# Dense products on scaled fp16 pairs instead of fp32r pairs, in an attention and MLP block on one core

## The chip, the cores and the metric

The kernel runs on one core of one Trainium2 chip. The time is device microseconds of one execution; the median of three runs is given. The core's engines work side by side, each through its own list of instructions in order: PE (matrix products into PSUM), ACT (functions with a scale and a bias), DVE (vectors), POOL (vectors, slower), and SP, which here issues all DMAs. They wait for each other by semaphores.

## The reference

```python
x  = A_x                                   # 1 x 2048 x 640, fp32
xn = _layernorm(x)
# attention, 32 heads of 20, each query sees itself and the 255 keys before it
qkv = (xn @ wqkv).reshape(1, 2048, 3, 32, 20)          # wqkv 640 x 1920
p = softmax(where(mask, (q @ k.T) * 20 ** -0.5, -1e9))
s = (p @ v).reshape(1, 2048, 640) @ wo                 # wo 640 x 640
# MLP on the same xn: w1 640 x 1536, w2 1536 x 640
r = relu(xn @ w1 + b1)
g = silu(r * r @ w2 + b2)
return x + s * g
```

All inputs and the output are fp32.

## The kernel before

**Pairs.** A dense product `a @ b` in fp32 is made of three PE products. Each operand is split into a high part, a rounded copy, and a low part, what is left of it; high x high, high x low and low x high are summed in PSUM. Before, both parts are `F32R` (fp32r, four bytes an element). ACT makes the high part (`AF.Copy`), DVE or POOL the low one (`tensor_sub`). The attention's own products (scores, values) use bf16 and fp16 parts and are not touched.

**Layout.** P = 128. The 2048 rows are NB = 4 blocks of BT = 512, NT = 16 tiles of 128. D = 640 is KC = 5 chunks of 128; F = 1536 is 12 chunks. `xT[p][b]` holds part p of the normalized, transposed x of block b. Large tiles come from the pool `bigp` (8 buffers of 128 x 2560 fp32).

**First stage** (lines 96 to 409). Block by block: x is loaded and normalized (`stats` L142, `normalize` L151), turned by PE (`tps`, L167 and L302), split into `xT` (L103, L104) and spilled to DRAM (`spill_x`). From it come k and q of head group 0 (`qk_group` L201, `qk_evac`), and v for all heads (`v_all`: products `vps` L243 of 320 columns, evacuated into `vt` by ACT L247 and L251 and DVE L248 and L252). The weights wv and the first wq, wk groups are split by ACT (L178) and POOL (L179).

**Attention stage.** 16 head pairs x 16 query tiles make 256 steps, written out in the loop at the end of the function. Step s issues the scores of one tile (`sps` L432) and their row maxima (DVE, `junk` L444), nine steps later the transposed scores (`stps` L476), exponentials (ACT L483), the window's edges (POOL L484, L486), the fp16 high part (ACT L491) and low part (DVE L497), and later the value products (`ops` L511). Between these, `fill()` takes dense products out of a generator, `filler()`, as many as a table of costs per product allows (`total`, `per`), so that they are spread evenly over the steps:

- q and k of groups 1 to 4: `qkps` L562, 480 products of 512 columns, evacuated at L734 to L739 into three staging tiles from `stgp` (8 buffers) and stored to `q_d`, `k_d`;
- the MLP in two halves of F, `hf` = 0, 1. For each half the 8 blocks of MT = 256 rows: the split x is loaded back (`load_xb`, tile `xb`), `hps` (L562) multiplies it with w1, ACT and DVE make the squared relu, POOL its low part (`hh`, L785), `yps` (L816, 320 columns) multiplies with w2. The first half's result goes to DRAM (`y_d[0]`) and is loaded and added in the second (`yin`).

Weights for the fill pass through `piece`, which loads a raw tile and splits it some steps later, one per step (`tick`); `ensure(tag)` forces the rest of a tag.

**Last stage.** The attention's output is turned and split (`oT`), multiplied with wo (`wops` L562, 320 columns), multiplied with silu(y) and added to x.

All engines are under `manual_schedule`: the order of the code is the order of each engine's list. Within a `v_all` tile the code is

```python
for c in range(KC):
    for xp, wp in ((0, 0), (0, 1), (1, 0)):
        n += 1
        nc.tensor.matmul(ps, xT[xp][b][:, ...], wv[wp][:, c, ...], ...)   # L243
nc.scalar.activation(dst[:, :, :, 0:DH], psv, AF.Copy)                     # L247
nc.vector.tensor_sub(r1, psv, dst[:, :, :, 0:DH])                          # L248
if late:
    late.pop()()            # the tile before: L251, L252
late.append(rest)
for _ in range(...):
    if jobs:
        jobs.pop(0)()       # statistics and normalization of block b + 2
```

Of the kernel before, what the change touches and what calls it, by code (L numbers as in the profile page):

```python
# [8 lines left out]
F32R = mybir.dt.float32r  # L9
# [5 lines left out]
P = 128  # L15
# [14 lines left out]
NFH = F // 2 // P  # L30
FHALF = F // 2
# [13 lines left out]


def f32(ap):
    return ap.bitcast(F32)
# [3 lines left out]
def attn_mlp_kernel(ctx: ExitStack, tc, x, wqkv, wo, w1, b1, w2, b2, out):  # L52
# [3 lines left out]
    bigp = ctx.enter_context(tc.tile_pool(name="bigp", bufs=8))  # L56
# [4 lines left out]


    xs_d = [[dram.tile([P, KC * BT], F32, name=f"xs{p}_{b}") for b in range(NB)] for p in range(2)]
# [12 lines left out]
    y_d = [dram.tile([P, NT, D], F32, name=f"y{i}") for i in range(2)]  # L76
# [21 lines left out]
    nc.gpsimd.memset(eps, EPS)  # L98
    b1t = const.tile([P, F // P], F32, name="b1t")
# [7 lines left out]
    xT = [[None] * NB for _ in range(2)]  # L107
# [19 lines left out]
    with tc.tile_pool(name="ph1v", bufs=2) as p1v, tc.tile_pool(name="ph1", bufs=2) as p1, tc.tile_pool(name="ph1x", bufs=4) as p1b, tc.tile_pool(name="ph1w", bufs=1) as p1w:  # L127
# [8 lines left out]

        wv = [p1w.tile([P, KC, D], F32R, name=f"wv{p}") for p in range(2)]

# [6 lines left out]
        def inv_std(rstd, var):  # L145
            nc.scalar.activation(rstd, var, AF.Sqrt, bias=eps)
            nc.vector.reciprocal(rstd, rstd)
# [5 lines left out]

        def alloc_x(b):
            for p in range(2):
                xT[p][b] = bigp.tile([P, KC * BT], F32R, tag="big", name=f"xT{p}_{b}")

        def spill_x(b):
            for p in range(2):
                nc.sync.dma_start(xs_d[p][b], f32(xT[p][b]))  # L160

        def transpose_chunks(b, xns):
            for c in range(KC):
# [4 lines left out]
                split(xT[0][b][:, c * BT:(c + 1) * BT], xT[1][b][:, c * BT:(c + 1) * BT], ps)  # L168
# [8 lines left out]
        def split_w(hi, lo, raw):  # L177
            nc.scalar.activation(hi, raw, AF.Copy)  # L178
            nc.gpsimd.tensor_sub(lo, raw, f32(hi))  # L179

        def group_tiles(g, w):
            return tuple(wgt.tile([P, KC, P], F32R, tag=f"wg{w}{q}", name=f"wg{w}{q}_{g}") for q in "hl")
# [12 lines left out]
        def qk_group(w, b, ps, t0=0, n=BT):  # L195
            hi, lo = ws0[w]
            m = 0
            for c in range(KC):
                for wt, part in ((hi, 0), (hi, 1), (lo, 0)):
                    m += 1  # L200
                    nc.tensor.matmul(ps, wt[:, c, :], xT[part][b][:, c * BT + t0:c * BT + t0 + n], start=m == 1, stop=m == 3 * KC)  # L201

        def qk_evac(w, b, ps, t0=0, n=BT):
# [3 lines left out]
            nc.scalar.activation(hm[:, 0, :], ps, AF.Copy)  # L207
            nc.vector.tensor_sub(rest, ps, hm[:, 0, :])
# [20 lines left out]
        def v_all(b, between=None):  # L229
            late = []  # L230
            jobs = norm_jobs(b + 2) if b + 2 < NB else []
            for nh in range(2):
# [3 lines left out]
                nc.gpsimd.memset(vt[:, :, :, :, VW - 1:VW], 1.0)  # L236
                for t in range(4):
                    ps = pmm.tile([P, HALF], F32, tag="mm", name="vps")
                    n = 0
                    for c in range(KC):  # L240
                        for xp, wp in ((0, 0), (0, 1), (1, 0)):
                            n += 1
                            nc.tensor.matmul(ps, xT[xp][b][:, c * BT + t * P: c * BT + (t + 1) * P], wv[wp][:, c, nh * HALF:(nh + 1) * HALF], start=n == 1, stop=n == 3 * KC)  # L243
# [12 lines left out]
                    for _ in range(0 if between and not nh else 2 if between else 1):  # L256
                        if jobs:
                            jobs.pop(0)()
                    store_all()
# [4 lines left out]
        with tc.manual_schedule(engines={E_.PE, E_.Activation, E_.DVE, E_.Pool, E_.SP}):  # L264
# [5 lines left out]
            ws0, ws1 = {}, {}  # L270
# [7 lines left out]
            views = [xT[p][0].rearrange("p (c n) -> p c n", c=KC) for p in range(2)]  # L278
            stats(xts[0][0], mv[:, 0, :])
            wjobs = []  # L280
            for w in "kq":
                ws0[w] = group_tiles(0, w)
                wjobs.append((*ws0[w], raws.pop(0)))
            firsts, seconds = [], []

            wvt = [bigp.tile([P, KC * BT], F32, tag="big", name=f"wvr{j}") for j in range(2)]
            wvr = [wvt[c // 3][:, c % 3 * D:(c % 3 + 1) * D] for c in range(KC)]
            for c in range(KC):
                nc.sync.dma_start(wvr[c], wqkv[c * P:(c + 1) * P, 2 * D:3 * D])
                wjobs.append((wv[0][:, c, :], wv[1][:, c, :], wvr[c]))  # L290

            def root(t):
                nc.scalar.activation(rstd[:, t:t + 1], mv[:, t, 1:2], AF.Sqrt, bias=eps)
# [16 lines left out]
            def rests(r):  # L310
                for ps, (hi, lo) in r:
                    nc.vector.tensor_sub(lo, ps, f32(hi))
# [16 lines left out]
            highs(t0_)  # L329
            stats(xts[0][2], mv[:, 2, :])  # L330
            root(2)
            rests(t0_)
            split_w(*wjobs.pop(0))
            t2_ = turned(2)
            highs(t1_)
            rests(t1_)
            split_w(*wjobs.pop(0))
# [7 lines left out]
            split_w(*wjobs.pop(0))  # L345
            highs(t3_)
            for _ in range(2):
                split_w(*wjobs.pop(0))
# [4 lines left out]
            for t in range(4):  # L353
                stats(xts[1][t], mv1[:, t, :])
# [5 lines left out]
            for f in firsts + seconds:  # L360
                if wjobs:
                    split_w(*wjobs.pop(0))
                lasts.append(qk_evac(*f))
                if len(lasts) == 2:
                    lasts.pop(0)()
            lasts.pop()()
            store_all()
            spill_x(0)
            nc.sync.dma_start(b1t, b1.rearrange("(c p) -> p c", p=P))
            nc.sync.dma_start(b2t, b2.partition_broadcast(P))  # L370
            ones_rows(0)
            for b in range(NB):
                def next_x():
                    if b + 1 < NB:
# [4 lines left out]
                        spill_x(b + 1)  # L379

                if b == 0:
                    inv_std(rstd1, mv1[:, :, 1])
                    xns = [normalize(xts[1][t], mv1[:, t, :], rstd1[:, t:t + 1]) for t in range(4)]
                    load_x(2)
                    raws = [load_w(group_src(1, w), KC) for w in "qk"]
                    v_all(b, next_x)
# [8 lines left out]
                next_x()  # L395
                if b == 1:
                    for w in "qk":
                        ws1[w] = group_tiles(1, w)
                        split_w(*ws1[w], raws.pop(0))
# [5 lines left out]
                v_all(b)  # L405
# [627 lines left out]
```

## Time and profile before

| | |
|---|---|
| median of 3 runs | 936.42 us (935.34 to 936.46) |
| profiled execution, first to last instruction | 933.0 us |
| PE busy | 907.9 us (97%) |
| DVE busy | 758.8 us (81%) |
| ACT busy | 670.1 us (72%) |
| POOL busy | 538.1 us (58%) |
| first stage | 0 to 120 us |
| attention stage with its fill | 120 to 852 us |
| last stage | 852 to 933 us |

No time is given for the profiled execution beside its span; the span is what its rows add up to. In a row of the profile `yps<-w,hh 128*128 128x320 f32 x1152 | 227.3, 331` means: 1152 products into `yps` with 128 rows and 320 columns, 227.3 us busy in all, 331 ns each from start to end. Products overlap, so the spacing of their starts is much smaller; it is read from runs of them in the chain that ended last. In a table of windows the number behind each engine's busy time is its count of instructions; "PEclk" is the granted PE clock, 1.00 being full speed.

### The profile page before, as it was taken

How to read it: one execution, taken by the hardware profiler on the slowest of the kernel's cores; microseconds unless marked ns; L12 is line 12 of the kernel's file. 1: busy time of each engine (PE TensorE's matmuls, PEld its weight loads, DVE VectorE, ACT ScalarE, POOL GpSimd, SP SyncE). 2: the span in 40 equal slices, each digit the busy share in tenths (PEclk: the TensorE clock that was granted, in tenths of full speed). 3: DMA queues.
4: the chain of work that ended last, by engine and by line, in shares of the span. 5: the costliest groups of instructions: out<-in, count | busy, mean ns of one | idle time of the engine just before them, and what ended most of it. 6: DMA issues, size and time to landing. Idle time of an engine off the chain costs nothing.

```text
span 933.0 us, 23236 instructions
## 1 busy us (share of the span) xinstructions
PE 907.9 (97%) x8352; PEld 792.4 (85%) x8352; DVE 758.8 (81%) x2031; ACT 670.1 (72%) x1282; POOL 538.1 (58%) x832
## 2 busy tenths in 40 slices
PE   8999999999998999999999999899999999999998
PEld 7899976666666798898899897798998898889998
DVE  7694478989999988888888889988888888866554
ACT  5354339888988887887887788887787888795221
POOL 6010017887878876866766775766775766782000
PEclk9999999999999999999999999999999999999999
DMA  6998686777789553343445266445354544128873
GB/s 230 307 398 301 207 265 195 225 223 234 231 252 307 180 164 94 116 141 99 142 122 150 74 193 204 150 150 161 113 163 141 159 131 143 56 74 280 292 276 124
DMA packets 150072, 174.11 MB, mean 187 GB/s; under 512 B 44420, under 2 KB 112068, under 8 KB 148932
## 3 DMA queue, kind: packets, MB, share of 16 engines
q1 hardware_dynamic: 149956, 172.63, 57.8%
q8 instruction: 65, 1.06, 0.5%
q14 instruction: 51, 0.42, 0.1%
HBM read 101.39 MB, written 70.91 MB: 185 GB/s over the span
## 4 chain that ended last, share of the span: by engine, by line
PE 71%; DVE 15%; ACT 4%; issue 4%; DMA 3%; POOL 2%; SPq 0%; POOLq 0%; DVEq 0%; ACTq 0%
PE yps L816 15%; PE hps L562 14%; PE wops L562 8%; PE sps L432 7%; PE vps L243 6%; PE stps L476 6%; PE ops L511 6%; PE qkps L562 5%; DVE junk L444 4%; DVE pl L497 3%; DVE w L659 2%; PE qkps L201 1%; ACT p L483 1%; ACT ph L491 1%; DVE st L142 1%
## 5 line engine op out<-in xcount | busy, mean ns | idle before, releaser
L483 ACT ACTIVATE p<-stps,ebias 128x384 f32<-128x384 f32 (+2 forms) x512 | 258.0, 556 | 89.7 <-PE stps L476 84.6
L444 DVE CUSTOM_DVE_ANT_0 junk<-sps,mask 128x384 bf16<-128x384 f32 (+2 forms) x512 | 251.0, 527 | 62.3 <-PE sps L432 55.9
L497 DVE TENSOR_TENSOR pl<-p,ph 128x768 f16<-128x768 f32 (+2 forms) x256 | 249.2, 973 | 1.8 <-ACT ph L491 1.7
L562 PE MATMUL hps<-xb,w 128*128 128x256 f32 x1440 | 230.8, 300 | 0.0
L816 PE MATMUL yps<-w,hh 128*128 128x320 f32 x1152 | 227.3, 331 | 0.0
L484 POOL TENSOR_SCALAR_AFFINE_SELECT p<-p 128x256 f32<-128x256 f32 x256 | 149.2, 583 | 120.9 <-ACT p L483 111.3
L491 ACT ACTIVATE ph<-p 128x768 f16<-128x768 f32 (+2 forms) x256 | 205.8, 804 | 13.4 <-POOL p L486 12.0
L562 PEld LDWEIGHTS hps<-xb,w 128*128 128x128 f32 x1440 | 194.6, 190 | 11.9 <-issue 2.1
L816 PEld LDWEIGHTS yps<-w,hh 128*128 128x128 f32 x1152 | 179.7, 189 | 11.8 <-issue 2.4
L432 PE MATMUL sps<-ks,qs 120*128 120x384 bf16 (+2 forms) x512 | 128.9, 319 | 8.1 <-DVE mt L444 7.8
L785 POOL TENSOR_TENSOR hh<-sq,hh 128x256 fp32r<-128x256 f32 x96 | 103.4, 1081 | 51.5 <-DVE sq L784 25.5
L476 PE MATMUL stps<-qs,ks 122*128 122x384 bf16 (+2 forms) x512 | 123.9, 322 | 1.0 <-ACT p L483 0.4
L486 POOL TENSOR_SCALAR_AFFINE_SELECT p<-p 128x256 f32<-128x256 f32 x224 | 111.9, 500 | 0.0
L511 PE MATMUL ops<-vp,ph 128*128 128x61 bf16 x1440 | 101.1, 193 | 0.0
L511 PE MATMUL ops<-vp,pl 128*128 128x61 bf16 x1440 | 99.8, 192 | 0.0
L511 PEld LDWEIGHTS <-ph 128*128 128x128 f16 x1440 | 86.0, 97 | 14.5 <-issue 7.4
L511 PEld LDWEIGHTS <-pl 128*128 128x128 f16 x1440 | 87.8, 98 | 0.0
L243 PE MATMUL vps<-wv,xT 128*128 128x320 f32 x480 | 72.1, 309 | 0.6 <-POOL wv L179 0.3
L243 PEld LDWEIGHTS vps<-wv,xT 128*128 128x128 f32 x480 | 70.5, 188 | 1.3 <-POOL wv L179 0.6
L562 PE MATMUL wops<-wo,oT 128*128 128x320 f32 x384 | 62.5, 311 | 0.3 <-DVE oT L104 0.3
L739 POOL TENSOR_TENSOR slo<-srt,shm 128x512 bf16<-128x512 f32 x32 | 39.5, 1236 | 37.7 <-PE sps L432 24.2
L432 PEld LDWEIGHTS <-qs 120*128 120x128 bf16 x512 | 36.3, 98 | 27.9 <-issue 13.7
(112 smaller groups left out, 1334.5 us busy)
## 6 DMA issues: line engine op xcount, KB each, us to landing
xb<-xs SPq DMA_DIRECT2D x32, 640.0 KB
ks<-k_d SPq DMA_DIRECT2D x64, 240.0 KB
qs<-q_d SPq DMA_DIRECT2D x64, 240.0 KB
xs<-xT SPq DMA_DIRECT2D x8, 1280.0 KB
y<-ysb SPq DMA_DIRECT2D x32, 320.0 KB
q_d<-shm SPq DMA_DIRECT2D x38, 256.0 KB
v_d<-vt SPq DMA_DIRECT2D x8, 976.0 KB
vp<-v_d SPq DMA_DIRECT2D x16, 488.0 KB
```

What stands on the lines that cost most here:

```text
L243: nc.tensor.matmul(ps, xT[xp][b][:, c * BT + t * P: c * BT + (t + 1) * P], wv[wp][:, c, nh * HALF:(nh + 1) * HALF], start=n == 1, stop=n = ...
L432: nc.tensor.matmul(ps[:, :nk], qs[i][0:KR, hh, q * P:(q + 1) * P], ks[i][0:KR, hh, k0 * P:k0 * P + nk], start=True, stop=True)
L444: nc.vector.tensor_tensor_reduce(out=junk[:, :nk], in0=r[hh][:, :nk], in1=mask[:, 3 * P - nk:], scale=1.0, scalar=-3.0e38, op0=ALU.add, op ...
L476: nc.tensor.matmul(ps[:, :n], ks[i][0:KR + 2, hh, kb * P:(kb + 1) * P], qs[i][0:KR + 2, hh, kb * P:kb * P + n], start=True, stop=True)
L483: nc.scalar.activation(p32[:, hh, :n], r[hh][:, :n], AF.Exp, scale=SCALE, bias=ebias)
L484: nc.gpsimd.affine_select(p32[:, :, 0:P], p32[:, :, 0:P], pattern=[[0, 2], [1, P]], compare_op=ALU.is_ge, fill=0.0, base=0, channel_multip ...
L486: nc.gpsimd.affine_select(p32[:, :, 2 * P:], p32[:, :, 2 * P:], pattern=[[0, 2], [-1, P]], compare_op=ALU.is_gt, fill=0.0, base=0, channel ...
L491: nc.scalar.activation(ph[:, :, :n], p32[:, :, :n], AF.Copy)
L497: nc.vector.tensor_sub(pl[:, :, :n], p32[:, :, :n], ph[:, :, :n])
L511: nc.tensor.matmul(ot[:, q % 4, hh, :], t[:, hh, (q - k) * P:(q - k + 1) * P], vp[:, k // 4, k % 4, hh, :], start=m == 1, stop=m == 2 * le ...
L562: nc.tensor.matmul(ps, a, b_, start=j == 0, stop=j == n - 1)
L816: nc.tensor.matmul(pss[nh], hs[fc][:, hp, tt * P:(tt + 1) * P], lin1(wt2, (wp * NFH + fc) * D + nh * HALF, HALF), start=fc == 0 and j == 0 ...
```

## The change

Every dense product takes both operands as fp16 pairs. Because fp16 has a small range, each weight matrix is first multiplied with a power of two worked out on the chip: ACT squares the raw weights and sums along rows (`accum_out`), PE sums over partitions with a matrix of ones (`totals`), DVE halves the exponent by a shift and inverts it (`weight_scale`), and POOL works out the factor that takes the scale off again (`past_x`). x is scaled by 2^11 within its normalization. Evacuations multiply with the inverse scale. For w1 the sums are also taken by column, and for w2 weighted by what the first layer will give (`mlp_scales`, `second_scales`).

What moves with it:

- `xT` is kept on chip as fp16 (`bigp` now 10 buffers); `spill_x`, `load_xb` and their DMAs go.
- All 12 chunks of F are done at once: 8 blocks of 12 x 15 `hps` and 4 x 36 `yps` products, 12 + 3 `hh` tiles; `y` is stored once, `yin` goes. The number of products stays.
- w1 is loaded, squared, scaled and split in the first stage; so are the sums for the q and k groups (`wgr`). w2 and wo are loaded in the attention stage once for their squares (17 pieces, tag `s`), and again to be split.
- wv is split by ACT and DVE, no longer by ACT and POOL. The statistics of block 1 stand behind that.
- `stgp` has 4 buffers instead of 8.
- fp16 weights are loaded into PE by an instruction of their own; fp32r products carry it in themselves.

```diff
-        nc.vector.tensor_sub(lo, src, f32(hi))
+        nc.vector.tensor_sub(lo, src, hi)
+    def split_s(hi, lo, src, sc):
+        nc.scalar.activation(hi, src, AF.Copy, scale=sc)
+        nc.vector.scalar_tensor_tensor(lo, src, sc, hi, ALU.mult, ALU.subtract)
...
+    def weight_scale(name, sums):
+        m = col(f"{name}_m")
+        n = sums.shape[-1]
+        if n > 1:
+            nc.vector.tensor_reduce(m, sums, axis=mybir.AxisListType.X, op=ALU.add)
+        nc.vector.tensor_scalar(m, m if n > 1 else sums, TINY, None, ALU.max)
+        inv = half_exponent(f"{name}_i", m)
+        sc = col(f"{name}_s")
+        nc.vector.tensor_scalar(inv, inv, 2.0 ** 49, None, ALU.mult)
+        nc.vector.reciprocal(sc, inv)
+        return sc, inv
...
+        def squares(acc, src):
+            sq = p1.tile([P, F], BF16, tag="sq", name="sq")[:, :src.shape[-1]]
+            nc.scalar.activation(sq, src, AF.Square, accum_out=acc)
+            return sq
+        def totals(c0, acc):
+            r = sums[:, c0:c0 + acc.shape[-1]]
+            nc.tensor.matmul(r, onesf, acc, start=True, stop=True)
+            return r
...
-        def split_w(hi, lo, raw):
-            nc.scalar.activation(hi, raw, AF.Copy)
-            nc.gpsimd.tensor_sub(lo, raw, f32(hi))
+        def split_w(hi, lo, raw, sc):
+            nc.scalar.activation(hi, raw, AF.Copy, scale=sc)
...
+            nc.gpsimd.tensor_scalar(scaled, raw, sc, 1.0, ALU.mult, ALU.mult)
+            nc.gpsimd.tensor_sub(lo, scaled, hi)
...
+            for c in range(KC):
+                squares(ssv[:, c:c + 1], wvr[c])
+            totv = totals(2, ssv)
...
+            def w1_squares(i):
+                c, o, n, ap = w1_raw[i]
+                sq = squares(ss1[:, i:i + 1], ap)
+                for f in range(o // P, (o + n) // P):
+                    nc.tensor.matmul(n2[:, f:f + 1], sq[:, f * P - o:(f + 1) * P - o], onesb, ...)
...
+                    v_all(b, next_x, [lambda: None] * 3 + [lambda c=c: squares(ssg[:, c:c + 1], wg_raw[c]) for c in range(KC)])
+                    totg = totals(8, ssg)
...
+                    more = [lambda i=i: w1_squares(i) for i in range(len(w1_raw))]
+                if b == 2:
+                    mlp_scales(totals(16, ss1), n2)
+                    w1t.extend(big(f"w1_{j}", F16) for j in range(3))
+                    more = [lambda r=r: w1_split(*r) for r in w1_raw]
...
-    stg = ctx.enter_context(tc.tile_pool(name="stgp", bufs=8))
+    stg = ctx.enter_context(tc.tile_pool(name="stgp", bufs=4))
+    hhp = ctx.enter_context(tc.tile_pool(name="hhp", bufs=15))
...
+            def go(raw, acc=acc):
+                sq = stg.tile([P, D], BF16, tag="stg", name="sq")
+                nc.scalar.activation(sq, raw, AF.Square, accum_out=acc)
+            piece("s", src, go)
```

In `v_all` each entry of `more` is called at the end of a tile, behind `jobs`.

Three places show what moves. On PE, the start of the program, from the warming transposes on (`tps` are the turned x, `qkps` the first k product). Before:

```order
L269 MATMUL warm_ps<-ident 128x128 x22
L302 MATMUL tps<-ident,xn 128x128 x5
L316 MATMUL warm_ps<-ident 128x128 x10
L302 MATMUL tps<-ident,xn 128x128 x5
L316 MATMUL warm_ps<-ident 128x128 x10
L302 MATMUL tps<-ident,xn 128x128 x5
L201 MATMUL qkps<-xT_0_175,wgkh_183 128x256
```

Now:

```order
L394 MATMUL tps<-ident,xn 128x128 x5
L408 MATMUL warm_ps<-ident 128x128 x10
L240 MATMUL sums<-ss_k,onesf 128x1
L394 MATMUL tps<-ident,xn 128x128 x5
L240 MATMUL sums<-ss_q,onesf 128x1
L277 LDWEIGHTS w0kh
L277 MATMUL qkps<-xT_171,w0kh 128x256
```

Two totals, for k and for q, now stand ahead of the first k product.

On ACT, the first stage in block 1 (`vt` are evacuations of v tiles, first part from `vps`, second from `r`; `xT` the turned x of the next block). Before:

```order
L103 ACTIVATE xT_2_753<-tps 128x512 x5
L178 ACTIVATE wgqh_800<-raw 128x640
L178 ACTIVATE wgkh_804<-raw 128x640
L247 ACTIVATE vt<-vps 128x8x2x20 x2
L251 ACTIVATE vt<-r_828 128x8x2x20
L247 ACTIVATE vt<-vps 128x8x2x20
L251 ACTIVATE vt<-r_847 128x8x2x20
```

Now:

```order
L103 ACTIVATE xT_842<-tps 128x512 x5
L107 ACTIVATE qkw<-raw,g_s 128x640 x2
L326 ACTIVATE vt<-vps 128x8x2x20
L235 ACTIVATE sq,ss_487<-w1r_786 128x1536
L326 ACTIVATE vt<-vps 128x8x2x20
L330 ACTIVATE vt<-r_912 128x8x2x20
L235 ACTIVATE sq,ss_487<-w1r_786 128x1024
L326 ACTIVATE vt<-vps 128x8x2x20
L330 ACTIVATE vt<-r_945 128x8x2x20
L235 ACTIVATE sq,ss_487<-w1r_787 128x512
```

A square of w1 now stands behind each tile's evacuation; PE's next 4 to 12 instructions behind that tile, the column sums, read it.

On ACT, early in the attention stage (`p` exponentials, `ph` their high part, `shm` evacuations of q and k). Before:

```order
L483 ACTIVATE p_1833<-stps,ebias 128x384 x2
L491 ACTIVATE ph<-p_1795 128x768
L738 ACTIVATE shm<-srt 128x512
L483 ACTIVATE p_1867<-stps,ebias 128x384 x2
L491 ACTIVATE ph<-p_1833 128x768
L734 ACTIVATE shm<-qkps 128x512
```

Now:

```order
L857 ACTIVATE shm<-srt 128x512
L795 ACTIVATE sq,ss_1749<-raw 128x640
L628 ACTIVATE p_2209<-stps,ebias 128x384 x2
L636 ACTIVATE ph<-p_2163 128x768
L853 ACTIVATE shm<-qkps,g_x 128x512
L795 ACTIVATE sq,ss_1749<-raw 128x640
```

A square of a w2 or wo piece, in a staging tile, now stands ahead of each step's exponentials.

More of the change, by code (lines that the diff above doesn't have):

```diff
@@ L662, in piece_pair @@
-    def piece_pair(tag, hi, lo, src):
-        def go(raw):
-            nc.scalar.activation(hi(), raw, AF.Copy)
-            nc.vector.tensor_sub(lo(), raw, f32(hi()))
-        piece(tag, src, go)
-    def lazy(make):
-        got = []
-        def get():
-            if not got:
-                got.append(make())
-            return got[0]
-        return get
     def queue_group(g):
         r = {}
-        for w in "qk":
-            hi = lazy(lambda w=w: wgt.tile([P, KC, P], F32R, tag=f"wg{w}h", name=f"wg{w}h_{g}"))
-            lo = lazy(lambda w=w: wgt.tile([P, KC, P], F32R, tag=f"wg{w}l", name=f"wg{w}l_{g}"))
+        for i, w in enumerate("qk"):
+            hi, lo = (qkw[0][:, g % 2, i, j] for j in range(2))
@@ L742, in filler @@
                     pending.append(evac)
[L743 to L761 removed]
+        shut.discard("22")
```

400 lines of the change are left out of this document (223 added, 177 removed).

## The prediction

> **What bounds the kernel now.** I read the page's engine totals first, then a table of windows cut where the stages change, then the chain that ended last, and only then single groups. Durations are those of one profiled execution with a span of 933.0 us; the median of the runs shown, 936.42 us, lies 3.4 us above it, and I add these 3.4 at the end.
>
> ```profile
> 0.00:120.00 120.00, 114.88 (x753) 109.13 (x754) 78.07 (x175) 54.13 (x122) 19.52 (x32) 1.00 0.83 287
> 120.00:282.00 162.00, 159.51 (x1246) 110.63 (x1246) 145.62 (x395) 132.57 (x240) 116.77 (x162) 1.00 0.75 234
> 282.00:322.00 40.00, 34.76 (x338) 27.43 (x335) 39.60 (x94) 35.11 (x68) 33.98 (x43) 1.00 0.74 242
> 322.00:553.00 231.00, 229.97 (x2412) 207.49 (x2411) 197.16 (x584) 184.65 (x356) 160.37 (x265) 1.00 0.44 134
> 553.00:602.00 49.00, 43.95 (x442) 37.41 (x440) 46.82 (x116) 42.11 (x81) 35.07 (x50) 1.00 0.53 162
> 602.00:813.00 211.00, 210.17 (x2227) 189.51 (x2226) 181.05 (x533) 169.59 (x327) 144.47 (x242) 1.00 0.44 135
> 852.00:933.00 81.00, 77.07 (x544) 76.75 (x542) 42.65 (x86) 18.82 (x30) 1.79 (x3) 1.00 0.65 226
> ```
>
> The columns after a window's length are PE, weight loads, DVE, ACT and POOL busy, granted clock, DMA share and GB/s. PE is busy throughout the first stage (to 120) and the last (from 852), and in the attention stage but for two stretches, 282 to 322 and 553 to 602, where PE idles 5.2 and 5.1 us and DVE is at 99% and 96%: there w1 and w2 are split. But DVE (85 to 90%) and ACT (80 to 82%) stand close behind PE.
>
> ```profile
> 408.62 0.34 PE stps L476 x2
> 408.97 1.43 PE hps L562 x12
> 410.40 0.34 PE sps L432 x2
> 410.74 0.59 PE hps L562 x5
> 411.33 0.34 PE stps L476 x2
> 411.67 0.83 PE hps L562 x7
> 412.50 0.70 PE ops L511 x24
> 413.21 0.16 PE sps L432
> 413.37 0.06 PE sps L458
> ```
>
> This piece of the chain is two steps of attention, and nothing but PE stands in it. It gives the price of a product: fp32r with 256 columns 1.43/12 = 0.119 us; with 16-bit operands 0.0292 for 61 columns (24 in 0.70), 0.06 for 128, 0.17 for 384.
>
> **The change part by part.** *Cheaper products.* Three rows give the other fp32r prices:
>
> ```profile
> 69.03 6.87 PE qkps L201 x30
> 78.08 17.60 PE vps L243 x120
> 856.51 8.80 PE wops L562 x60
> ```
>
> 512 columns take 0.229 us, 320 take 0.1467: 0.4286 ns a column, and 9.6 ns over the columns' time at 256, 320 and 512 alike. The 16-bit rows, at the same 0.4286, are 3.0, 5.1 and 5.4 ns over. So an fp16 product should save 4.2 to 6.6 ns; I take 5.5, with ends 9.6 (nothing over) and 1.6 (8 over, were the 0.34 a full 0.345). The attention stage has 1440 + 1152 + 480 = 3072 such products: 16.9 us on PE. With DVE and ACT so near, I count 12 of it as time. In the first stage, 480 vps and 120 qkps: 3.3 us; behind 852, 480 wops: 2.6 us.
>
> The Trainium skill has a lower price (TensorE: Matmul & The Clock Gate, Back-to-back issue gap: columns over 2.4 GHz plus about 2.5 ns once warm), which is 109, 136 and 216 ns here; no fp16 row of this size is in the trace. By it the three terms would be some 24, 7 and 5 us, and the sum some 18 us lower, about 937.
>
> *Less beside the path.* The spill of x, the 32 xb loads, half of the y traffic, the yin loads and 32 of 64 ysb additions (0.475 us each, 15 us of DVE) go. PE was waiting for none of them in the rows above, so I count nothing beyond the 12 us; what covers them is PE's own work, and they make room on DVE. Of the two splitting stretches the second goes (5.1 us saved, taken as 5). The first stays: twelve w2 pieces of 640 replace five w1 and six w2 pieces.
>
> *The first stage pays.* PE, ACT and DVE run in the written order, so whatever is queued behind a wait waits too.
>
> ```profile
> L178 ACT ACTIVATE wv<-wvr 128x640 fp32r<-128x640 f32 x5 | 3.5, 740 | 0.0
> L900 ACT ACTIVATE yb<-yb 128x1280 f32<-128x1280 f32 x8 | 10.3, 1286 | 0.0
> L247 ACT ACTIVATE vt<-vps 128x320 bf16<-128x320 f32 x32 | 14.4, 451 | 33.3 <-PE vps L243 33.2
> L251 ACT ACTIVATE vt<-r 128x320 bf16<-128x320 f32 x32 | 15.2, 476 | 7.0 <-DVE r L248 7.0
> L448 DVE TENSOR_SCALAR mp<-mt 128x8 bf16<-128x8 f32 x64 | 14.0, 219 | 2.2
> L665 DVE TENSOR_TENSOR wo<-raw,wo 128x640 fp32r<-128x640 f32 x4 | 3.9, 984 | 0.0
> L142 DVE BATCH_NORM_STATS2 st<-xt 128x6 f32<-128x320 f32 x32 | 13.8, 474 | 8.9 <-DMA xt<-in_A_x_dram 8.9
> L151 DVE TENSOR_SCALAR xn<-xt,mv,rstd 128x640 f32<-128x640 f32 x16 | 9.4, 623 | 0.3
> 22.43 6.97 PE vps L243 x45
> 49.34 2.09 PE tps L167 x17
> ```
>
> ACT takes 0.85 ns an element (from 740 and 1286): a sum of squares over 640, 1280, 1536 costs 0.74, 1.29, 1.5 us.
>
> (a) Start. For k, then q: a square (0.74), a ones-product on PE (some 0.3), four small DVE operations (0.2 each), ACT's copy, and a second 640-wide POOL operation ahead of the subtraction. I get the last first-group product at 18 us instead of 15.6. Then PE holds the v total in front of the second groups: five squares (3.7) must come first, so these run from 21.6 to 24.9, not 15.6 to 19.2. The ten wv halves follow, one on ACT and one on DVE (5 x 0.98) between eight small DVE evacuations of 0.4: wv is whole near 30. And the four pairs of statistics (4.2) and four xn (2.2), which used to lie before, now stand on DVE ahead of the first vps evacuation, near 37.5; with three PSUM buffers the fourth vps tile waits. First half of v done near 40, before 29.4 (22.43 + 6.97): 10 us.
>
> (b) Second half of v. ACT gets five squares of 1280 among evacuations; the g total stands on PE behind the last, which waits for evacuation, rest, square: about 2.2 us on ACT per tile against PE's 2.2, plus what wgr lands late. I put the g total at 56 to 59, so another 6 us; the wait of 2.1 us for the next xn before the chain's 49.34 goes. Net 4.
>
> (c) Seven pieces of w1 squares in block 1. PE's 60 column sums stand between vps tiles. After a tile PE waits for ACT's vt (0.45), the rest of the tile before (0.48) and the square (0.5 to 1.5): seven times about 1.1 plus 7680 x 0.85 ns = 6.5, plus 60 x 0.03: 16 us. Nothing hides this; it is PE's own queue.
>
> (d) Scales and w1 split in block 2: DVE adds some 16 x 0.2 and 7680 elements at 1.04 ns, 11 us, which three PSUM buffers just about cover: 1 us.
>
> Sum 31 us. If the squares came from ACT for half of that, 15; if wgr and w1 also land late, 38.
>
> *The attention stage pays.* The 17 pieces of squares cost ACT 0.74 each, one per step, in steps 7 to 23, where ACT is already at 82% of 2.8 us: 6 us longer. The second scales: PE waits for two POOL multiplications behind its queue, and DVE does ten small operations: 2 us. The staging tiles of q and k go from 8 buffers to 4, shared with the squares:
>
> ```profile
> 164.64 4.52 DMA k_d<-shm
> 208.83 4.02 DMA k_d<-slo
> ```
>
> A store takes 4 to 4.5 us to land. In the written order eight buffers were reused some four steps after the store was issued, four are reused one to two steps after; a step is (813 - 120)/256 = 2.7 us long. Engines waiting for a landing hold what is queued behind them, ACT its exponentials and POOL its selections. I take 3 us; the ends are 0 and 32 evacuations x 1.5 = 48. Sum 11 us.
>
> Sum: 933 - 12 - 3.3 - 2.6 - 5 + 31 + 11 = 952, and 3.4 gives 955.
>
> **The rivals.** *The step is PE's alone* (faster). Everything but PE has room in the attention stage, so both idle stretches vanish (10.3), squares and stores cost nothing, and each product's saving counts in full: 933 + 31 - 10.3 less 22.8 (at 5.5 ns) or 39.9 (at 9.6) = 931 or 914; with 3.4, 917 to 934. For it: PE at 99.6% from 322 to 553. Against: DVE is at 90% from 120 to 282. It decides once the stage gives back over 25 us.
>
> *The staging ring* (slower still). Each of 32 evacuations stops an engine for 1.5 us: 955 + 45 = 1000; half of it, 978. For it: the two landings above stand in the chain that ended last. Against: a q store lands sooner, and POOL has slack.
>
> *The gaps cool PE.* New waits of about 3 and 6 us stand ahead of the v and g totals.
>
> ```profile
> 1.74 3.97 PE L269 MATMUL warm_ps<-ident 128*128 128x128 f32 x22 [1.74 <-POOL ident L82]
> 7.25 1.25 PE L316 MATMUL warm_ps<-ident 128*128 128x128 f32 x10
> ```
>
> The first 22 transposes take 0.18 us each, ten later ones 0.125, though the granted clock reads 1.00 in all windows. If both gaps are followed by 3 us at such a pace, 2 to 4 us are lost: 958. The Trainium skill (TensorE: Matmul & The Clock Gate, Part 1: The HAM clock gate) says that an idle window of about 3.4 us halves the clock, which the second gap would bring about; the trace of before has no PE gap of that length behind its first microseconds, and cannot show it.
>
> **How the numbers follow.** The forecast, 940 to 970 with the first stage 24 to 38 us longer: 0.60. PE alone: 0.20. Staging ring: 0.12. Cooled PE: 0.08. Leaving out the lower half of the PE rival and the upper half of the ring's leaves the range 925 to 982. A measurement of this kernel can tell about 0.2%, 1.9 us, from no change. Faster: 0.19 of the PE rival and 0.03 of the forecast's low end, 0.22; within 0.2%, 0.06; slower 0.72.
>
> **What would show it.** Right: first scores near 148 us instead of 120; PE idle behind ACT's squares in front of the column sums, seven times 1.5 to 2.7 us; fp16 products of 256 columns spaced 0.113 to 0.115; steps of about 2.65 us between 350 and 800. Wrong: first scores by 135; or steps at 2.55 with DVE and ACT keeping up, which is the PE rival; or waits for q_d and k_d landings on ACT, DVE or POOL of over 15 us, which is the ring.

## The result and the profile after

| | before | after |
|---|---|---|
| median of the runs, us | 936.44 (935.34 to 936.64, 4 runs) | 976.59 (974.51 to 982.2, 4 runs) |
| ratio, 95% interval | 1 | 1.0443 (1.0411 to 1.0475) |
| span of the profiled execution, us | 933.0 | 980.5 |
| PE busy, us | 907.9 | 896.6 |
| mean granted clock | 1.000 | 0.963 |

The change makes the kernel 40 us slower; 18.6 had been forecast. The profiled execution is the slowest of the four, so the two spans differ by 47.5 us, and the parts below add up to that. PE is busy 11 us less, although part of its work now runs at a lower clock, and it idles 84 us instead of 25.

A window table, cut at the first score products, the 65th of the 256 attention steps, the last scores and the first wops product. Columns as in the prediction. Before:

```profile
0.00:120.00 120.00, 114.88 (x753) 109.13 (x754) 78.07 (x175) 54.13 (x122) 19.52 (x32) 1.00 0.83 287
120.00:289.40 169.40, 165.23 (x1291) 114.36 (x1291) 153.02 (x409) 138.40 (x251) 121.88 (x167) 1.00 0.76 238
289.40:818.30 528.90, 518.42 (x5416) 462.72 (x5412) 461.78 (x1321) 429.41 (x825) 371.54 (x597) 1.00 0.47 143
818.30:850.00 31.70, 30.29 (x329) 27.57 (x327) 22.47 (x40) 27.35 (x55) 23.37 (x34) 1.00 0.45 152
850.00:933.00 83.00, 79.07 (x574) 78.65 (x574) 43.48 (x88) 20.79 (x32) 1.79 (x3) 1.00 0.66 230
```

The same five parts after, the first stage in three rows:

```profile
0.00:72.40 72.40, 52.82 (x321) 37.29 (x322) 45.47 (x117) 36.34 (x80) 11.46 (x33) 0.88 0.74 247
72.40:117.00 44.60, 29.51 (x183) 16.66 (x181) 17.48 (x39) 16.97 (x36) 0.94 (x2) 0.67 0.27 92
117.00:166.90 49.90, 48.73 (x323) 31.79 (x322) 34.05 (x69) 28.38 (x54) 7.77 (x13) 0.99 0.54 173
166.90:372.80 205.90, 175.40 (x1301) 88.90 (x1299) 155.84 (x422) 154.68 (x286) 115.36 (x170) 0.94 0.75 227
372.80:871.00 498.20, 488.36 (x5426) 376.55 (x5423) 436.31 (x1279) 434.20 (x822) 356.08 (x600) 1.00 0.29 82
871.00:902.90 31.90, 28.13 (x314) 20.59 (x313) 21.49 (x35) 25.11 (x46) 19.22 (x30) 1.00 0.43 138
902.90:980.50 77.60, 73.64 (x574) 55.33 (x573) 47.05 (x88) 22.58 (x32) 1.62 (x3) 1.00 0.67 237
```

First stage +46.9; the first 64 steps +36.5; the other steps -30.7; between +0.2; last stage -5.4. So both the loss and the gain are larger than forecast. The clock column has a second message: 0.88, 0.67 and 0.94 in the rows that lost most, 1.00 in those that gained.

The gain, in the chain that ended last (start, time, and how many products the row holds):

```profile
353.31 1.51 PE qkps L707 x7
431.81 1.36 PE yps L906 x10
452.04 1.31 PE hps L707 x12
...
927.35 8.15 PE wops L707 x60
```

An fp16 product takes 0.2157 us (512 columns), 0.136 (320) and 0.109 (256), against 0.229, 0.1467 and 0.119 before. The formula of the Trainium skill (TensorE: Matmul & The Clock Gate, Back-to-back issue gap: columns over 2.4 GHz plus about 2.5 ns, given there for an isolated product) comes to 0.216, 0.136 and 0.109, and the trace agrees, here in unbroken runs of products.

The loss in block 1 of the first stage, on PE's timeline (idle time before a row and who ended it stand in brackets):

```profile
72.38 2.20 PE L322 MATMUL vps<-wv,xT 128*128 128x320 f16 x15
78.24 0.48 PE L502 MATMUL sums<-onesb,sq 128*128 128x1 bf16 x12 [3.66 <-ACT sq L235]
78.58 4.16 PE L322 MATMUL vps<-wv,xT 128*128 128x320 f16 x15
84.66 0.38 PE L502 MATMUL sums<-onesb,sq 128*128 128x1 bf16 x8 [1.92 <-ACT sq L235]
84.90 4.16 PE L322 MATMUL vps<-wv,xT 128*128 128x320 f16 x15
90.56 0.26 PE L502 MATMUL sums<-onesb,sq 128*128 128x1 bf16 x4 [1.50 <-ACT sq L235]
...
102.21 0.25 PE L502 MATMUL sums<-onesb,sq 128*128 128x1 bf16 x4 [1.19 <-ACT sq L235]
102.33 2.20 PE L322 MATMUL vps<-wv,xT 128*128 128x320 f16 x15
106.63 0.35 PE L502 MATMUL sums<-onesb,sq 128*128 128x1 bf16 x8 [2.11 <-ACT sq L235]
106.85 3.43 PE L322 MATMUL vps<-wv,xT 128*128 128x320 f16 x15
```

Between two v tiles PE waits for a square, and the tile behind the wait takes 3.4 to 4.16 us instead of 2.20; only the one behind the shortest wait, 1.19 us, takes 2.20. Over the whole program the longest waits on PE, by what ended them, are:

```profile
PE stps L621 <- ACT p L628: 17.0, 17, 2.7
PE sps L577 <- DVE mt L589: 15.4, 30, 4.2
PE sums L502 <- ACT sq L235: 15.1, 7, 3.7
PE sums L240 <- ACT sq L235: 6.8, 3, 4.0
```

(total us, times, longest.) What held ACT and POOL in the first 64 steps, from their waits between 167 and 373:

```profile
...
ACT shm L853 <- POOL slo L858: 7.3, 3, 5.8
ACT sq L795 <- DMA k_d<-shm: 7.2, 3, 3.3
...
ACT sq L795 <- DMA q_d<-shm: 2.5, 1, 2.5
```
```profile
...
POOL slo L858 <- DMA q_d<-slo: 13.8, 3, 10.4
POOL slo L858 <- ACT shm L857: 12.2, 7, 4.2
```

A square that wants a staging tile waits until a store of q or k out of that tile has landed; `slo` does too. In the chain that ended last ten such landings stand between 167 and 373, 2.1 to 6.75 us each and 45 us in all, where before it held the two that the prediction shows. Two of the ten:

```profile
178.45 6.75 DMA q_d<-shm
270.18 6.75 DMA k_d<-shm
```

### The profile page after: what moved, and what is told of

The parts are those of the page before. It is cut to its first block, busy times and chain, and to the rows that moved or that the text cites. A ratio compares the mean times of both kernels' runs of the same rounds, so it can differ in the third digit from the quotient of the medians.

```text
span 980.5 us, 23410 instructions
## 1 busy us (share of the span) xinstructions
PE 896.6 (91%) x8426; PEld 627.1 (64%) x8426; DVE 757.7 (77%) x2045; ACT 718.3 (73%) x1351; POOL 512.4 (52%) x851
## 4 chain that ended last, share of the span: by engine, by line
PE 52%; ACT 15%; DVE 8%; DMA 7%; issue 5%; POOL 2%; SPq 0%; POOLq 0%; ACTq 0%; DVEq 0%
PE yps L906 14%; PE hps L707 9%; PE wops L707 7%; ACT p L628 6%; PE ops L656 5%; PE sps L577 5%; PE stps L621 5%; ACT ph L636 3%; DMA k_d<-shm 3%; PE vps L322 3%; DVE junk L589 3%; PE qkps L707 2%; ACT relu L879 2%; DVE pl L642 2%; POOL slo L858 1%
## 5 line engine op out<-in xcount | busy, mean ns | idle before, releaser
L636 ACT ACTIVATE ph<-p 128x768 f16<-128x768 f32 (+2 forms) x256 | 205.9, 804 | 4.4 <-POOL p L631 2.7
L707 PE MATMUL hps<-xT,w 128*128 128x256 f16 x1440 | 191.3, 272 | 0.0
L906 PE MATMUL yps<-w,hh 128*128 128x320 f16 x1152 | 188.9, 298 | 0.0
L707 PEld LDWEIGHTS <-w 128*128 128x128 f16 x1440 | 139.1, 97 | 40.8 <-issue 5.9
L906 PEld LDWEIGHTS <-hh 128*128 128x128 f16 x1152 | 110.8, 97 | 52.6 <-issue 3.0
L707 PE MATMUL qkps<-xT,qkw 128*128 128x512 f16 x480 | 132.0, 399 | 0.0
L883 POOL TENSOR_TENSOR hh<-sq,hh 128x256 f16<-128x256 f32 x96 | 101.8, 1061 | 45.0 <-DVE sq L882 23.6
L322 PE MATMUL vps<-wv,xT 128*128 128x320 f16 x480 | 82.1, 337 | 7.4 <-DVE xT L104 3.0
L707 PEld LDWEIGHTS <-qkw 128*128 128x128 f16 x480 | 48.2, 101 | 53.4 <-issue 17.0
L621 PEld LDWEIGHTS <-ks 122*128 122x128 bf16 x512 | 50.3, 98 | 44.8 <-issue 21.2
L322 PEld LDWEIGHTS <-xT 128*128 128x128 f16 x480 | 51.6, 109 | 33.6 <-issue 8.6
```

The source lines that it names most:

```text
L322: nc.tensor.matmul(ps, xT[b][:, xp, c, t * P:(t + 1) * P], wv[wp][:, c, nh * HALF:(nh + 1) * HALF], start=n == 1, stop=n == 3 * KC)
L621: nc.tensor.matmul(ps[:, :n], ks[i][0:KR + 2, hh, kb * P:(kb + 1) * P], qs[i][0:KR + 2, hh, kb * P:kb * P + n], start=True, stop=True)
L636: nc.scalar.activation(ph[:, :, :n], p32[:, :, :n], AF.Copy)
L707: nc.tensor.matmul(ps, a, b_, start=j == 0, stop=j == n - 1)
L883: nc.gpsimd.tensor_sub(hh[:, 1], sq, hh[:, 0])
L906: nc.tensor.matmul(pss[nh], hs[fc][:, hp, tt * P:(tt + 1) * P], lin1(w2t, (2 * fc + wp) * D + nh * HALF, HALF), start=fc == 0 and j == 0, ...
```

## Experiments

Theory: the change's products save what their spacing shows, and three costs eat it: waits on statistics in PE's queue, the slower clock behind such waits, and a staging ring half as long that the squares share. Rivals: the lower clock only shows the waits and costs nothing itself; the squares cost by ACT's time, not by the ring; the losses hide one another. All kernels are edits of the changed kernel. "64 steps" is the time from the first score product to that of the 65th step in the profiled execution. The last two columns come from one execution each, so they scatter: after, sqraw, ring5 and nosq2 have the same first stage, and their first scores come at 166.9, 167.1, 165.5 and 162.2, with a granted clock of 0.86, 0.86, 0.88 and 0.89 up to there.

The ring in its old length with the squares in it was not measured: with 8 buffers in `stgp` the changed kernel has 9.69 KB a partition left on chip, and `hhp` needs 15. What the ring costs is read from sqraw, ring5 and nosq2.

| run | median, us | first scores at | 64 steps |
|---|---|---|---|
| before | 935 to 936 | 120.0 | 169.4 |
| after | 976.59 | 166.9 | 205.9 |
| warm | 969.97 | 157.2 | 201.6 |
| lag | 955.36 | 140.7 | 205.2 |
| laglateg | 949.78 | 139.5 | 201.9 |
| nosq1 | 936.0 | 124.9 | 202.9 |
| sqraw | 965.65 | 167.1 | 195.7 |
| ring5 | 959.07 | 165.5 | 189.0 |
| nosq2 | 958.74 | 162.2 | 186.4 |
| allout | 905.37 | 121.8 | 174.0 |
| both | 932.84 | 137.1 | 187.5 |
| both2 | 928.41 | 136.2 | 183.0 |
| both3 | 924.87 | 137.6 | 180.6 |

### PE kept busy in the waits (warm)

```
                 sq = squares(ss1[:, i:i + 1], ap)
+                fill = pat.tile([P, P], F32, tag="s", name="fill")
+                for _ in range(28 if i == 0 else 16):
+                    nc.tensor.transpose(fill, ident, ident)
                 for f in range(o // P, (o + n) // P):
```

> In block 1 of the first stage PE gets 28 transposes of the identity ahead of the first group of column sums and 16 ahead of each of the other six: 124 more instructions of 0.107 us, 13 us of PE time that computes nothing, in the places where PE waited for ACT's squares (15.1 us in seven waits). Theory (the cold clock): the six v tiles that took 3.4 to 4.2 us there instead of 2.2 go back to 2.2, so block 1 gets 8 to 11 us shorter and the whole comes to 965 to 969 us, although PE has more to do. Rival (the waits alone cost the time, and the granted clock only reports them): no change within 2 us, or up to 5 us slower by the transposes that outlast the waits.

Block 1, from its first v tile to the next k product, takes 34.6 us instead of 44.6, as the theory said. The median is 6.6 us lower, 969.97 (967.22 to 974.83), just short of the theory's 965 to 969 and outside the rival's. The PE timeline, in the place shown above:

```profile
75.19 3.27 PE L503 MATMUL fill<-ident 128*128 128x128 f32 x28
78.93 0.45 PE L505 MATMUL sums<-onesb,sq 128*128 128x1 bf16 x12 [0.46 <-ACT sq L235]
79.25 2.20 PE L322 MATMUL vps<-wv,xT 128*128 128x320 f16 x15
```

The first column sums begin 0.7 us later than in the changed kernel, and yet the tile behind them is back at 2.20 us, as are all later ones. Instructions that compute nothing made the kernel faster, so here the clock is a cost of its own and no mere sign of the waits.

### Column sums one tile later (lag)

```
+                if colsums:
+                    colsums.pop()()
+                colsums.append(lambda: w1_columns(i, c, o, n, sq))
+
+            def w1_columns(i, c, o, n, sq):
                 for f in range(o // P, (o + n) // P):
...
```

> The column sums of a w1 piece stand one v tile later in PE's queue (behind the next tile's products), squares on ACT stay where they are. Theory (PE's order): PE no longer waits behind the squares, 15.1 us in seven waits go and with them the slow clock of the tiles behind (some 11 us); block 1 from 72.4 to 117 shrinks to about 20 to 24 us, first scores at 143 to 147 instead of 167, the whole 953 to 958. Rival (ACT is the bound there, or w1's pieces land late): the waits move to the next tile, and under 10 us come back, 967 or more.

Median 955.4, in the theory's range; first scores at 140.7, a little earlier than its 143 to 147. So 26 us of the 47 in the profiled executions, 21 us by the medians, come from where seven short groups of instructions stand in one queue. On its PE timeline the tiles follow each other:

```profile
77.04 2.20 PE L322 MATMUL vps<-wv,xT 128*128 128x320 f16 x15
79.08 0.34 PE L509 MATMUL sums<-onesb,sq 128*128 128x1 bf16 x8
79.28 2.20 PE L322 MATMUL vps<-wv,xT 128*128 128x320 f16 x15
```

ACT does the same squares; PE no longer needs each at once. ACT was not the bound.

### The g total later too (laglateg)

```
-                    totg = totals(8, ssg)
...
                 if b == 1:
+                    totg = totals(8, ssg)
```

> As the run with the column sums one tile later (955.4), and the total and scale of the groups are put behind the k and q products of block 1 in PE's queue, where nothing in front of block 1's turned groups needs them. Theory (every wait in PE's queue costs itself and the slow clock behind it): the wait of 4.0 us in front of the g total and the fifteen products at 0.42 to 0.63 us behind it go; first scores at 132 to 136 instead of 140.7, the whole 947 to 951. Rival (PE would have waited there for the x of block 1 or for PSUM buffers anyway): under 3 us, 953 or more.

The whole came out in the theory's range (949.8), but not by its reason: first scores moved by 1.2 us only, where 5 to 9 were expected, so the hit is in part luck. A wait of 3.7 us before the first column sums took the place of the one removed (lag had 1.6 us there):

```profile
72.86 0.48 PE L509 MATMUL sums<-onesb,sq 128*128 128x1 bf16 x12 [3.71 <-ACT sq L235]
73.21 4.16 PE L322 MATMUL vps<-wv,xT 128*128 128x320 f16 x15
```

The 64 steps, which the edit does not touch, are 3.3 us shorter, 2.7 of it in steps 40 to 56; these take 50.9 to 55.9 us over the runs that compute everything, so it may be scatter, and why the median fell by 5.6 is open.

### No statistics in the first stage (nosq1)

```
-            nc.tensor.matmul(r, onesf, acc, start=True, stop=True)
+            r = fixed[:, c0:c0 + acc.shape[-1]]
...
-            nc.scalar.activation(sq, src, AF.Square, accum_out=acc)
...
-                for f in range(o // P, (o + n) // P):
```

> All sums of squares of the first stage (k, q, v, the groups, w1), their totals and the column sums are left out, constants stand in their place; the small DVE operations that make scales of the totals, the splits and the order of the rest stay. It gives what the scales of the first stage cost in all. Theory (the waits on the statistics and the clock that they cool make the whole +47 us): first scores at 118 to 128 us, the whole 930 to 938. Rival (the statistics of block 1 and the normalising put ahead of the v tiles, and the split of wv, cost a large part): first scores at 135 to 145, the whole 945 to 955. The steps of the attention stage do not change by either.

First scores at 124.9 and 936.0 in all (930.73 to 940.12), both in the theory's ranges. Of 46.9 us in the first stage, 42.0 go with the statistics and their totals. The attention steps keep their loss (202.9).

### The squares off the ring (sqraw)

```
-                sq = stg.tile([P, D], BF16, tag="stg", name="sq")
-                nc.scalar.activation(sq, raw, AF.Square, accum_out=acc)
+                nc.scalar.activation(raw, raw, AF.Square, accum_out=acc)
```

> The 17 squares of w2 and wo in the attention stage write their unused output over the raw piece itself instead of a buffer of the staging pool, which stays at 4 buffers. Measured against the changed kernel (976.6; the 64 first steps take 205.9 us there and 169.4 before). Theory (the ring: a square's output tile waits until a store of q or k has landed, and ACT with its exponentials behind it): the waits of the squares for landings (11.6 us between 167 and 410) go, the 64 first steps take 188 to 196 us, the whole 960 to 968. Rival (the squares' ACT time, 17 times 0.8 us, or the four buffers that the q and k tiles themselves need): under 4 us come back, 972 or more.

64 steps 195.7 (10.2 less), 965.7 in all, both in the theory's ranges. ACT does the same squares; only where their unused output goes has changed. Among its ACT waits in these steps, no square waits for a store any more, while the q and k tiles still do:

```profile
ACT shm L852 <- DMA k_d<-slo: 3.5, 2, 2.2
...
ACT raw L794 <- DMA raw<-in_B_w_dram: 1.5, 2, 0.8
```

### A longer ring besides (ring5)

```
-    stg = ctx.enter_context(tc.tile_pool(name="stgp", bufs=4))
+    stg = ctx.enter_context(tc.tile_pool(name="stgp", bufs=5))
...
-                        lo = stg.tile([P, BT], BF16, tag="stg", name="slo")
+                        lo = hhp.tile([P, BT], BF16, tag="hh", name="slo")
```

> As the run with the squares over the raw piece, and besides the low part slo of each q and k tile is put into the pool of hh tiles, idle at that time, and the staging pool has 5 buffers: 2.5 evacuations in flight instead of 1.33 (before 2.67). Theory (the ring): the 64 first steps come to 170 to 180 us, the whole to 942 to 953. Rival (ACT's squares and the first stage's backlog): 960 or more, and no better than the run with the squares alone moved by more than 4 us.

Both of the theory's numbers missed: 189.0 instead of 170 to 180, and 959 instead of 942 to 953. That is 6.6 us better than sqraw, more than the rival allowed, though the four runs spread from 955 to 964. The first eight steps fell from 21.9 to 17.4 us (before: 16.6), but steps 8 to 24 rose from 49.4 to 54.3, since one of them took 9.3 us:

```profile
185.50 5.82 DMA raw<-in_B_w_dram
...
191.40 0.77 ACT raw L794 x2
```

With the ring out of the way, ACT came to a square before its piece had landed, and its exponentials stood behind. The loads of the squares are a cost that neither side had named.

### No squares of w2 and wo (nosq2)

```
-                        queue_squares()
+                        nc.gpsimd.memset(ss2, 1.6)
+                        nc.gpsimd.memset(sso, 1.6)
```

> The 17 squares of w2 and wo and the loads of their pieces are left out (constants stand in their place), the second scales stay; the staging pool has 4 buffers. It tells what the squares cost in all, ring and ACT time together. Theory (the ring, with q and k tiles among its users): 64 first steps 182 to 190 us, the whole 955 to 964; the difference to the run with the squares over the raw piece, ACT's time alone, is 3 to 8 us. Rival (ACT's time is what the squares cost): this run 10 us or more below that one.

64 steps 186.4, 958.7 in all, both in the theory's ranges; the run is 6.9 us below sqraw, less than the rival's 10. In the 64 steps the squares cost 19.5 us, 10.2 of them through the ring, the other 9.3 by their loads and ACT's time together, which no run separates.

### Both groups of statistics out, longer ring (allout)

The edits of nosq1 and nosq2, and of ring5 the 5 buffers and the `slo` in the hh pool.

> All squares, totals and column sums of the first stage left out as in the run without them (936.0), the 17 squares of w2 and wo left out too, slo in the hh pool and 5 staging buffers: the fp16 products and the x that stays on chip with hardly any of what the scales cost. Theory (the products gain about 31 us, the rest of the change is cost of the first stage and of the ring): the 64 first steps 170 to 180 us instead of 202.9, the whole 903 to 913, faster than before by 22 to 32. Rival (the two losses hide one another, or the earlier start of the stage runs into the transfers): 920 or more.

905.4, ratio to before 0.968 (0.9658 to 0.9702), 64 steps 174.0. The products, the x that stays on chip and all else that is left gain 30 us on the kernel before, and the squares, their totals and the short ring cost the changed kernel 71 us. The rival's 920 or more did not come.

### The repairs together (both, both2, both3)

`both` is the edits of laglateg and ring5 together.

> The repairs together: column sums one tile later, g total behind the next products, squares over the raw piece, slo in the hh pool, 5 staging buffers; nothing is left out of the computation. Theory (the losses lie in different places and add): 976.6 less 26.8 less 17.5 is 932; 928 to 937, first scores at 137 to 141, 64 first steps 184 to 190. Rival (they overlap, since the stage that starts earlier finds the same transfers under way): 940 or more.

932.8 where 932 had been added up: the losses of the first stage and of the ring add, and do not hide one another. The ratio to before is 0.9988 (0.9973 to 1.0002), no difference.

```
+                    more = [lambda: None] + [lambda i=i: w1_squares(i) for i in range(len(w1_raw))]
...
+            if not force and (tag in shut or state[2] < at_ + (4 if tag == 's' else AGE)):
...
+            if n == 1:
+                queue_squares(True)
```

(`queue_squares(True)` queues the five squares of wo alone; wo's scale moves with them.)

> As the repairs together, with three more moves: the w1 squares start one v tile later (the first waited 3.7 us for its piece to land), the squares of w2 are released only four steps after their load was issued instead of two (one such wait made a step of 9.3 us), and the five squares of wo with their scale come in the MLP part instead of at the start of attention. Theory (what is left are engines held by late loads): first scores 134 to 137, 64 first steps 176 to 184, the whole 919 to 929. Rival (the loads land late wherever they stand, and the wo squares now cost in the MLP steps): within 3 us of the run before it.

928.4, ratio 0.9929 (0.9916 to 0.9941). The longer age works: steps 8 to 24 went from 54.2 to 47.0. The w1 squares' shift brought next to nothing (first scores 136.2 for 137.1), since PE now waits 3.3 us for the first of them in the new place; the wo squares cost 3.6 us in the MLP steps (80 to 160: 210.8 instead of 207.2).

```
+            for _ in range(20):
+                nc.tensor.transpose(fill, ident, ident)
             totv = totals(2, ssv)
...
                     ensure(f"2{j}")
+                queue_squares(True)
```

The second fill is made like that of warm.

> As the last run (928.4), with two places filled and one move: 20 transposes of the identity ahead of the v total and 24 ahead of the first column sums (PE waited there 2.7 and 3.3 us, and the 30 products behind the first and the 15 behind the second ran at 0.21 and 0.24 us instead of 0.11 and 0.147), and the five squares of wo come in the y part of the first MLP block, where ACT has 2.0 us of work in a step of 2.55, instead of the h part of the second. Theory (a wait costs itself and the slow clock behind it, and a full engine passes a delay on): 1.5 and 1.4 us from the clock, 3.6 us from the 80 steps in which the wo squares stood, so 921 to 925. Rival (the groups behind the total wait for the split of wv and of w1 in any case, so that warmer products end in the next wait, and ACT is late in the y part too): within 2 us, 927 to 930.

924.9, ratio 0.9892 (0.9876 to 0.9909), in the theory's range, but by one of its two halves. Steps 80 to 160 are back at 207.2. The fills together moved nothing: first scores at 137.6 (136.2 before them). Behind the first fill the next wait grew, and with it the 45 products behind that (1.84 and 6.27 us in both2):

```profile
49.45 8.69 PE L322 MATMUL vps<-wv,xT 128*128 128x320 f16 x45 [4.04 <-DVE xT L104]
```

So at the v total the rival was right: the products ended sooner and waited for DVE, and these 45 begin at 49.45 with the fill and at 49.12 without. In block 1 the theory was: the tile behind the second fill takes 2.20 us instead of 3.60. This kernel computes everything, and is 1.1% faster than the kernel before and 5% faster than the changed one.

## Why the prediction was wrong, step by step

Direction and places were right: slower, through the first stage and the early attention steps, while the later steps gain. The size was not: 976.6 lies above the 940 to 970 of the likeliest case and near the upper end of the range, and the move is over twice the forecast one.

In the profiled execution the forecast adds 19.1 us and the measurement 47.5, so 28.4 are missing. The first stage lost 46.9 where 27.7 was forecast (31 less 3.3 of products). The attention stage with its fill lost 6.0 where a gain of 6 was forecast (11 less 12 and 5). The last stage gained 5.4 for 2.6. Two steps failed above all: the 11 us for squares, second scales and staging ring, where the 64 first steps lost 36.5; and the slow clock behind the waits, which the sum held at nothing, and which took 10.4 us in block 1 alone. The products' saving was put at half its size. That covered part of the miss, so it is partly luck that the time still lies in the range.

**The products** (16.9 us on PE in the attention stage, 12 counted). They saved 1440 x 10.0 + 1152 x 10.7 + 480 x 13.3 ns, 33 us on PE, twice the estimate. What failed here is the 5.5 ns, which I took from 61- to 384-column rows as an excess over a slope of 0.4286 ns a column fitted on fp32r rows; fp16 has a smaller slope, (0.2157 - 0.109)/256 = 0.417. The lower price weighed beside it was right. Of the saving, most counts as time: steps 80 to 255 without the former splitting stretch take 18.6 us less, 0.117 a step, and that stretch, 16 steps, fell from 51.0 to 40.2. "A spacing of 0.113 to 0.115" and "steps of 2.65" were wrong; "steps at 2.55", which I had given to the PE rival, came (median 2.54 with hps, 2.57 with yps; 2.70 and 2.71 before). As that rival said, the stage's later part did give back over 25 us (30.7). It fell because its condition was tied to the stage as a whole, and the 64 first steps lost more.

**(c), seven waits for squares** (16 us forecast). The waits are 15.1 us, as worked out. What was missing is the clock: the eight tiles of block 1 take 28.0 us by the timeline, 2.20, 4.16, 4.16, 3.80, 3.87, 2.20, 3.43 and 4.16, where eight at 2.20 are 17.6. The 10.4 us between them stand beside the 15.1 of the waits, so block 1 alone lost 26.9 (44.6 from its first v tile to the next k product, 17.7 before). I had priced cooling at 2 to 4 us for two gaps, in a rival of its own with 0.08, and had not applied it to the very waits that (c) counted; warm shows that it belongs there. The Trainium skill (TensorE: Matmul & The Clock Gate, Part 1: The HAM clock gate) has half the clock after an idle window of about 3.4 us; the trace agrees with the half (4.16 against 2.20, granted clock 0.67 in the window), but here, behind a first wait of 3.66 us, waits of 1.5 to 2.4 us between tiles were enough to keep it there, and behind the tile at 2.20 one of 2.11 us brought it back.

**(a) and (b)** (14 us forecast). The first half of v, four tiles of block 0, was done at 41.3 instead of the 40 that I had put (11.9 us lost for 10), the g total at 60.4 instead of 56 to 59. Block 1's first v tile begins at 72.38; before, it began at 51.19:

```profile
51.19 17.84 PE L243 MATMUL vps<-wv,xT 128*128 128x320 f32 x120
```

That is 21.2 us for 14, and most of the slip lies behind the first half of v. The clock stands at 0.88 up to 72 us, which these steps had not counted either. In the changed kernel:

```profile
22.47 0.59 PE L240 MATMUL sums<-ss_v,onesf 128*128 128x5 f32 x2 [2.69 <-ACT sq L235]
...
39.12 2.20 PE L322 MATMUL vps<-wv,xT 128*128 128x320 f16 x15 [1.33 <-DVE r L327]
```

The twelve products of 256 columns behind the first of these, the v total, take 2.5 us by the timeline (22.92 to 25.43), 0.21 each for 0.109; behind the g total the first products of 512 columns take 0.42 each for 0.2157.

**The staging ring** (3 us, with ends 0 and 48; squares 6, second scales 2). It is the largest miss: +36.5 in the 64 steps for 11. Squares and ring cost 28.9 of it by nosq1 against allout (202.9 and 174.0); 3.0 went with the first stage's statistics, within the scatter. What is left, 4.6, is in steps 40 to 56 (51.8 in allout, 43.3 before), where the second scales stand, PE's wait for which is the 2.0 us forecast, and w2's splits now lie; before, the splits began at step 58, and steps 56 to 64 are shorter now (20.6 for 24.1). The clock may have a share in the 28.9 too: it stands at 0.94 over the 64 steps, which is up to 12 us of 205.9 by my estimate (0.06 x 205.9), and at 1.00 in allout. No run fills the waits there, so how much of that costs time is open. I had taken the ring near its lower end because a q store lands sooner than a k store and POOL has slack; in the chain now a q store took 6.75 us to land. What I had not seen is that a square is one more user of the ring on ACT, ahead of the exponentials, and that 17 loads of 320 KB come into the same steps. My own test, waits of over 15 us for q_d and k_d landings, was met: 9.7 us on ACT's squares and 13.8 on POOL's slo in the rows above, 23.5 in all. So the forecast joined two rivals that both were partly true, at 0.12 and 0.08, as if only one could be.

**The last stage** (2.6) gave 5.4, by the same spacing. **The second splitting stretch** (5) gave about 9 beyond the products: 10.8 less 16 x 0.117. **Less beside the path, nothing**: no run takes the removed traffic and additions back in, so what they are worth by themselves stays open.

## What to carry over

Before a statistic goes into a program with in-order engines, look at which queue its reader stands in: 60 one-column products that read the squares, placed one tile too early, cost 21 us of median, and the same squares on ACT stayed when they moved. Price a wait on PE as the wait and the slower products behind it together. A scratch output, though nobody reads it, is a user of its pool: seventeen tiles in a ring that waits for stores cost 11 us of median, and writing them over a dead buffer took these away.

## What was not expected of the hardware

The granted clock fell with short waits: behind one of 2.69 us products of 256 columns took 0.21 us for 0.109, and 1.5 to 2.4 us of idleness in every 6 kept 15 products of 320 columns at 3.4 to 4.16 us. 124 transposes whose result nobody reads brought them back to 2.20. A sum that ACT collects beside its output is an instruction of its own, which I had not counted:

```profile
L795 ACT ACTIVATION_READ_ACCUMULATOR sq<-raw 128x1 f32 x17 | 3.4, 199 | 0.0
```

36 squares have such a row behind them, 0.2 us each.
